# Moving three softmax normalisations on VectorE's list around the steps of a recurrence

## The chip, the cores and the metric

One core of one Trainium2 chip. The metric is the device time of one execution in microseconds (us); lower is better. The time before is the median of three runs, 133.39 us (132.92 to 133.72).

## The reference

Two branches run on separate inputs of 2048 tokens by 448 features, and their outputs are joined along the last axis. Branch A is dilated local attention with 16 heads of 28 features, a window of 8 keys at a step of 2. Branch B is a diagonal complex recurrence over the 2048 tokens, between two projections, with a skip product.

```python
def _A_ref(x, wqkv, wo):
    ...
    logits = jnp.where(mask[None, None, :, :], logits, -1e9)
    attn = _softmax(logits, axis=-1)
    o = jnp.einsum("bhsw,bhswd->bhsd", attn, vg)
    return (lambda x, *d: x.transpose(*d))(o, 0, 2, 1, 3).reshape(B, S, D) @ wo

def _B_ref(x, Lambda_re, Lambda_im, B_re, B_im, C_re, C_im, log_dt, Dskip):
    ...
    for t in range(L):
        h = Lam_bar[None, :] * h + Bu[:, t, :]
        hs.append(h)
    hseq = jnp.stack(hs, 1)
    y = 2.0 * jnp.einsum("blp,dp->bld", hseq, Cmat).real + x * Dskip[None, None, :]
    return y
```

## The kernel before

Tokens are handled in pairs (even, odd), so that 1024 pairs remain; they are cut into 8 blocks of 128 for the attention and into two halves of 512 for the recurrence. Every piece of work is a named step, and one hand-written string, `ORDER`, lists all steps in the order in which they are issued. A name ends in a letter for the engine (P TensorE, V VectorE, A ScalarE, G GpSimd, S SyncE's queue) and for many in the number of a PSUM unit, U0 to U3. Each engine works through its own steps strictly in the order of that string and waits, instruction by instruction, for what the data need. A step that stands later on an engine's list therefore cannot overtake one that waits. In the profile PE is TensorE, DVE VectorE, ACT ScalarE, POOL GpSimd and SP SyncE.

The steps that matter here:

- **Attention.** `s{b}{p}` are the logits of block b (lines 645 and 649; 655 and 661 for the block of borders, b = 8), `x{b}{p}` the exponential on ScalarE (671, 673), `a{b}{p}` the products with the values (680, 682), which end in a unit U0 or U1. `n{b}` on VectorE normalises: a reciprocal of the sums (691) and a product (692) that reads the PSUM unit and writes the tile O. Only then is the unit free for TensorE's next step in it. `ot{b}` is a DMA transposition of O on SyncE's queue (698, 701); `w{t}f` and `w{t}t` are the output projection (362, 360) from the transposed tile.
- **Recurrence.** `b{k}{h}` computes the input of component pair k in half h (727), `be` copies it to the tile u. `ri{k}{h}` rotates it on VectorE: two products with cosine and sine into ra and rb (742, 743), then a sum and a difference into rv (744, 745). `sc{k}{h}{i}` are two scans over rv into rs (755). `ro{k}{h}` rotates back into the tile h (764 to 767). ra, rb, rv and rs have one buffer each.
- **Output of B.** `g0`, `g1`, `g2` (782, 784) with `ge0`, `ge1`, `gp2` on ScalarE and `ge2` on VectorE (819) build the small matrix Gm. `xd{t}` on VectorE (841) writes the skip product, which reads the tile xo, into the PSUM unit to which `y{t}` on TensorE (851, 854) then adds. xo comes by two transfers that GpSimd issues in the step `xol` (908, 909), which stands in the string well ahead of its first reader, xd1.
- **GpSimd and ScalarE** scale rows of the second projection (`tc..`, line 534 on GpSimd), and `c..` on VectorE (540) adds the other half; GpSimd's next piece waits for a buffer that such a `c` step frees.

Between 47 us and the end of the attention VectorE's list runs, in the order of the string: n0, c24, ri00, n1, c23, c21, two scans, c22, n2, ro00, c25, ri20, and so on to n3, the c steps, ro20, ri11, n4, c26, sc110, n5, ge2, xd1, n8, sc111, xd0, ro11, ri21, sc210, n6. On TensorE the same stretch ends with y1, s61, y0, a60, a61, s70, w3t, w3f, w0f: w0f writes the unit that n6 reads.

The steps involved, in the code:

```python
rc = rcs[0:n, 2 * b:2 * b + 2, :]
av = U[u_][:, :, 0:29 * H].rearrange("p t (h c) -> p t h c", c=29)
V.reciprocal(rc, av[0:n, :, :, 28])
V.tensor_tensor(O[0:n, :].rearrange("p (t h d) -> p t h d", t=2, h=H), av[0:n, :, :, 0:DH],
                rc.unsqueeze(3).to_broadcast((n, 2, H, DH)), ALU.mult)
```

Of the kernel before, what the change touches and what calls it, by code (L numbers as in the profile page):

```python
# [10 lines left out]
ALU = mybir.AluOpType  # L11
# [6 lines left out]
HALF = 512  # L18
# [26 lines left out]
n8.V1 y1.P0 sc111.V ot8.S xd0.V1 ro11.V s61.P y0.P1 x61.A ri21.V ye1.A0 yo1.S oc0.A a60.P0 sc210.V ye0.A1 yo0.S a61.P0
s70.P n6.V0 w3t.P1 x70.A w3f.P1 sc211.V ot6.S w0f.P0 we3.A1 wo3.S ro21.V w0t.P0 oc1.A s71.P we0.A0 wo0.S w4f.P1 x71.A
ri31.V w5f.P0 w5t.P0 w4t.P1 sc310.V w1t.P2 we4.A1 wo4.S w2t.P3 w1f.P2 we5.A0 wo5.S xd3.V1 w2f.P3 ro31.V we1.A2 wo1.S
a70.P0 we2.A3 wo2.S a71.P0 xd2.V2 y3.P1 n7.V0 xd5.V3 ot7.S ri01.V y2.P2 ye3.A1 yo3.S sc010.V oc2.A sc011.V w6f.P0
# [105 lines left out]
def kernel(  # L154
# [17 lines left out]
    V, ACT, PE, G, SP = nc.vector, nc.scalar, nc.tensor, nc.gpsimd, nc.sync  # L172
# [6 lines left out]
    def t_(shape, dt, name, tag=None):  # L179
        return sb.tile(shape, dt, tag=tag or name, name=name)  # L180
# [5 lines left out]
    u = t_([128, 7, HALF], BF16, "u")  # L186
# [13 lines left out]
    tab = t_([128, 2, 4, HALF], BF16, "tab")  # L200
# [342 lines left out]
    for m in range(7):  # L543
        o = m % 4 if m != 3 else 3
# [165 lines left out]
    def hbuf():  # L710
        if "h" not in lazy:
            lazy["h"] = t_([128, 7, NP + 4], BF16, "h", "rB")
            V.memset(lazy["h"][:, :, 0:1], 0.0)
# [4 lines left out]
    rv = [t_([128, 2, HALF], BF16, f"rv{i}") for i in range(1)]
    rs = [t_([128, 2, HALF], BF16, f"rs{i}") for i in range(1)]
    for hf in range(2):  # L720
        for k in range(4):
            ms = (k, k + 4) if k < 3 else (3,)

            def f(e, u_, ms=ms, hf=hf):
                for j, m in enumerate(ms):
                    for i in range(7):
                        PE.matmul(U[u_][:, j, :], WT[:, i, 128 * m:128 * m + 128], xB[:, i, HALF * hf:HALF * hf + HALF], start=(i == 0), stop=(i == 6))  # L727
            step[f"b{k}{hf}"] = f

            def f(e, u_, k=k, ms=ms):  # L730
                if k < 3:
                    evac(e, u[:, k:k + 5:4, :], U[u_])
                else:
                    evac(e, u[:, 3, :], U[u_][:, 0, :])
            step[f"be{k}{hf}"] = f

            def f(e, u_, k=k, hf=hf):
                c, s = tab[:, 0, k, :], tab[:, 1, k, :]
                v = rv[0]
                if k < 3:  # L740
                    up = u[:, k:k + 5:4, :]
                    V.tensor_tensor(ra[:], up, c.unsqueeze(1).to_broadcast((128, 2, HALF)), ALU.mult)
                    V.tensor_tensor(rb[:], up, s.unsqueeze(1).to_broadcast((128, 2, HALF)), ALU.mult)
                    V.tensor_tensor(v[:, 0], ra[:, 0], rb[:, 1], ALU.add)
                    V.tensor_tensor(v[:, 1], ra[:, 1], rb[:, 0], ALU.subtract)
                else:
                    V.tensor_tensor(ra[:, 0], u[:, 3, :], c, ALU.mult)
                    V.tensor_tensor(ra[:, 1], u[:, 3, :], s, ALU.mult)
                    V.tensor_tensor(v[0:64, 0], ra[0:64, 0], ra[64:128, 1], ALU.add)
                    V.tensor_tensor(v[64:128, 0], ra[64:128, 0], ra[0:64, 1], ALU.subtract)  # L750
            step[f"ri{k}{hf}"] = f
            for i in range(len(ms)):
                def f(e, u_, k=k, hf=hf, i=i):
                    m = k + 4 * i
                    V.tensor_tensor_scan(rs[0][:, i], p["r2"][:, k:k + 1].to_broadcast((128, HALF)), rv[0][:, i],  # L755
                                         0.0 if hf == 0 else ini[:, m:m + 1], ALU.mult, ALU.add)
# [157 lines left out]
    flag = t_([1, 1], I32, "flag")  # L914
# [65 lines left out]
```

## Time and profile before

| | us |
|---|---|
| median of three runs | 133.39 |
| the profiled execution | 133.22 |
| its span, first to last instruction | 131.4 |
| TensorE busy | 124.2 |
| VectorE busy | 107.1 |
| ScalarE busy | 86.7 |
| GpSimd busy | 48.1 |

The profiled execution's time holds some 1.8 us outside the span. A row of the list in order of time reads: start, length, engine, line, operation, written tile and read tiles, shapes, number of instructions merged into the row; in brackets the idle time of the engine ahead of it and who ended that. A row of a window reads: its bounds and length, the busy time of each engine with its count of instructions, the granted clock of TensorE (1.00 in all windows shown), the share of the 16 DMA engines in use, and GB/s. A row on a transfer ends with its size and the time from issue to landing. Busy times of neighbouring rows overlap slightly, since instructions are pipelined.

### The profile page before, as it was taken

Reading aid. Unit: us, or ns where it says so; the run is one execution under the profiler, and the core shown is the slowest. Engines: PE = TensorE matmul, PEld = TensorE weight load, DVE = VectorE, ACT = ScalarE, POOL = GpSimd, SP = SyncE. Lnnn points to the kernel's source line nnn. Section 1 sums busy time; section 2 is a strip of 40 time slices with the busy share of each in tenths; the row PEclk is TensorE's granted clock in tenths of the full one; section 3 lists DMA queues with packets and bytes.
Section 4 is the critical chain, followed back from the end, with each engine's and each line's share of the span. In section 5 each row is a group of like instructions: output and inputs, shape, how many; then the busy total and the mean of one; then the engine's idle time right before and its main releaser. Section 6 shows DMA issues by size and latency. Waiting matters only on the chain.

```text
span 131.4 us, 3138 instructions
## 1 busy us (share of the span) xinstructions
PE 124.2 (94%) x1226; PEld 63.5 (48%) x1226; DVE 107.1 (81%) x225; ACT 86.7 (66%) x91; POOL 48.1 (37%) x75
## 2 busy tenths in 40 slices
PE   7999999999999999899999998799999999999970
PEld 2654443443444466454445556545644654445540
DVE  2467999999898999999998999999999999870000
ACT  3348878987999879968698967608697523222230
POOL 7998900799851906560077850000000000000000
PEclk9999999999999999999999999999999999999999
DMA  4999998899779995898879967990452652422222
GB/s 98 373 299 223 246 114 164 121 250 204 166 120 200 227 134 86 157 205 200 178 159 148 203 123 260 181 205 14 138 145 71 209 145 70 140 70 72 70 72 80
DMA packets 54594, 20.83 MB, mean 158 GB/s; under 512 B 46830, under 2 KB 54208, under 8 KB 54576
## 3 DMA queue, kind: packets, MB, share of 16 engines
q1 hardware_dynamic: 53424, 18.70, 68.1%
q0 software_dynamic: 656, 1.50, 4.1%
q10 hardware_dynamic: 496, 0.40, 0.9%
q8 instruction: 11, 0.18, 0.6%
q14 instruction: 7, 0.06, 0.2%
HBM read 5.30 MB, written 3.86 MB: 70 GB/s over the span
## 4 chain that ended last, share of the span: by engine, by line
PE 62%; DVE 23%; issue 5%; DMA 3%; POOL 2%; ACT 1%; SPq 0%; DVEq 0%
PE U L362 16%; PE U L851 11%; PE early L362 8%; PE U L727 6%; PE late L851 4%; PE U L854 3%; PE U L360 3%; DVE O L692 3%; DVE natW L540 3%; DMA Wt<-in_A_wqkv_dram 3%; DVE C L540 3%; DVE rs L755 2%; POOL wtmp L534 2%; PE late L362 2%; PE early L360 2%
## 5 line engine op out<-in xcount | busy, mean ns | idle before, releaser
L671 ACT ACTIVATE P<-s 128x1920 bf16<-128x1920 f32 (+1 forms) x16 | 28.6, 1785 | 5.7 <-PE s L649 5.6
L727 PE MATMUL U<-xB,WT 128*128 128x512 bf16 x98 | 22.3, 380 | 0.0
L362 PE MATMUL U<-Wt,xA 128*128 128x448 bf16 x90 | 19.9, 355 | 0.7 <-DVE O L692 0.4
L362 PEld LDWEIGHTS <-xA 128*128 128x128 bf16 x144 | 12.9, 98 | 14.9 <-issue 4.4
L335 ACT CAST ys<-U 128x896 bf16<-128x896 f32 (+1 forms) x11 | 9.5, 871 | 12.0 <-PE U L851 9.2
L534 POOL TENSOR_SCALAR wtmp<-CT,p_pah 128x448 f32<-128x448 bf16 x6 | 12.6, 2107 | 11.2 <-DVE natW L540 6.4
L851 PEld LDWEIGHTS <-h 128*128 128x128 bf16 x105 | 10.0, 98 | 9.2 <-DVE U L841 0.2
L727 PEld LDWEIGHTS <-WT 128*128 128x128 bf16 x98 | 9.2, 98 | 10.7 <-DMA xB<-in_B_x_dram 0.2
L362 PE MATMUL early<-Wt,xA 128*128 128x448 bf16 x54 | 11.8, 354 | 0.0
L335 ACT CAST u<-U 128x1024 bf16<-128x1024 f32 (+1 forms) x8 | 7.2, 905 | 4.6 <-PE U L727 4.5
L692 DVE TENSOR_TENSOR O<-U,rcs 128x896 bf16<-128x896 f32 (+1 forms) x9 | 9.8, 1091 | 0.3
L851 PE MATMUL U<-natW,h 128*128 128x448 bf16 x42 | 9.0, 353 | 0.1
L755 DVE TENSOR_TENSOR_SCAN rs<-p_r,rv 128x512 bf16<-128x512 f32 x7 | 9.0, 1304 | 0.0
L755 DVE TENSOR_TENSOR_SCAN rs<-p_r,ini,rv 128x512 bf16<-128x512 f32 x7 | 8.8, 1275 | 0.0
L680 PE MATMUL U<-Vt,P 128*128 128x29 bf16 x256 | 8.2, 176 | 0.6 <-DVE O L692 0.6
L680 PEld LDWEIGHTS <-P 128*128 128x128 bf16 x256 | 7.6, 96 | 2.0 <-issue 0.7
L335 ACT CAST ys<-late 128x896 bf16<-128x896 f32 (+2 forms) x6 | 4.3, 718 | 6.1 <-PE late L851 5.6
L362 PE MATMUL U<-wo,OT 128*128 128x448 bf16 x36 | 7.6, 353 | 0.0
L851 PE MATMUL U<-C,h 128*128 128x448 bf16 x35 | 7.4, 353 | 0.0
L534 POOL TENSOR_SCALAR wtmp<-CT,p_pag 128x448 f32<-128x448 bf16 x2 | 4.2, 2081 | 8.4 <-DVE C L540 8.4
L339 DVE COPY Wt<-Wt 64x1344 bf16<-64x1344 bf16 (+1 forms) x5 | 3.7, 736 | 4.1 <-DMA Wt<-in_A_wqkv_dram 4.1
L335 ACT CAST Nx<-U 128x896 bf16<-128x896 f32 x7 | 6.4, 908 | 1.0 <-PE U L360 1.0
(198 smaller groups left out, 233.9 us busy)
## 6 DMA issues: line engine op xcount, KB each, us to landing
out_dram<-ys SPq DMA_DIRECT2D x12, 224.0 KB, 2.5
tmpB<-in_A_x_dram SPq DMA_DIRECT2D x4, 224.0 KB, 3.6
xo<-in_B_x_dram POOLq DMA_DIRECT2D x1, 896.0 KB, 6.7
out_dram<-ys SPq DMA_DIRECT2D x7, 112.0 KB, 1.8
Wt<-in_A_wqkv_dram SPq DMA_DIRECT2D x1, 672.0 KB, 6.0
wo<-in_A_wo_dram SPq DMA_DIRECT2D x2, 336.0 KB, 4.4
natW<-in_B_B_re_dram SPq DMA_DIRECT2D x1, 336.0 KB, 6.0
natW<-in_B_B_im_dram SPq DMA_DIRECT2D x1, 336.0 KB, 7.3
```

Of the source, the lines that this page charges most:

```text
L335: ACT.copy(o, i)
L360: PE.matmul(ps(u_)[j], x()[r, 3, c], w()[r, 3], start=first, stop=not first, skip_group_check=True)
L362: PE.matmul(ps(u_)[j], x()[:, 4 * j + k, c], w()[:, 4 * j + k], start=(k == 0 and first), stop=(k == 2 and not first), skip_group_check=True)
L534: (G if e == "G" else V).tensor_scalar(view(held_t[name][:]), src(), scale(), None, ALU.mult)
L540: V.scalar_tensor_tensor(view(dst()), src(), scale(), view(t[:]), ALU.mult, ALU.add)
L671: ACT.activation(pv[:, :, :, c0:128], s4[:, :, 0:4 * n].rearrange("p g (s q) -> p g s q", s=4), ACTF.Exp, scale=SCALE)
L680: PE.matmul(U[u_][:, q, 29 * hd:29 * hd + 29], P[:, hd // 4, hd % 4, :], Vt[:, b, q, hd, :], start=(hd == 0), stop=(hd == H - 1), skip_gro ...
L692: V.tensor_tensor(O[0:n, :].rearrange("p (t h d) -> p t h d", t=2, h=H), av[0:n, :, :, 0:DH], rc.unsqueeze(3).to_broadcast((n, 2, H, DH)), ...
L727: PE.matmul(U[u_][:, j, :], WT[:, i, 128 * m:128 * m + 128], xB[:, i, HALF * hf:HALF * hf + HALF], start=(i == 0), stop=(i == 6))
L755: V.tensor_tensor_scan(rs[0][:, i], p["r2"][:, k:k + 1].to_broadcast((128, HALF)), rv[0][:, i], 0.0 if hf == 0 else ini[:, m:m + 1], ALU.m ...
L851: PE.matmul(ps[:, 0:D], hb[:, m, lo:lo + 128], C1()[:, m, :] if par else natW[:, m, 0:D], start=(m == 0 and par == 0), stop=(m == 6 and pa ...
L854: PE.matmul(ps[:, 0:D], xB[:, k, tk], Gm[:, k, :], start=False, stop=(k == 3), skip_group_check=True)
```

## The change

The string `ORDER` is changed at three places, and one step, ri00, is cut in two so that another can stand between its halves. On TensorE, ScalarE, GpSimd and SyncE the lists are the same as before, instruction for instruction; all that moves is on VectorE.

```diff
-s11.P tc23.G n0.V1 k5t.P0 x11.A k5f.P0 wtx2.S c24.V a10.P1 ri00.V tc21.G qt3.S ke5.A0 s20.P a11.P1 x20.A q7t.P0 xb1.S
-q7f.P0 n1.V1 s21.P qe7.A0 c23.V
+s11.P tc23.G n0.V1 k5t.P0 x11.A k5f.P0 wtx2.S c24.V a10.P1 rp00.V tc21.G qt3.S ke5.A0 s20.P a11.P1 x20.A q7t.P0 xb1.S
+q7f.P0 n1.V1 rq00.V s21.P qe7.A0 c23.V
...
-a41.P1 ge1.A0 s51.P ri11.V g0.P0 x51.A n4.V1
-s80.P ge0.A0 c26.V ot4.S a50.P1 sc110.V x80.A a51.P1 wol.S g2.P0 n5.V1 gp2.A0 s60.P ge2.V0 x60.A a80.P1 ot5.S xd1.V0
-n8.V1 y1.P0 sc111.V ot8.S xd0.V1 ro11.V
+a41.P1 ge1.A0 s51.P g0.P0 x51.A n4.V1 ri11.V
+s80.P ge0.A0 c26.V ot4.S a50.P1 x80.A a51.P1 wol.S g2.P0 n5.V1 gp2.A0 s60.P ge2.V0 x60.A a80.P1 ot5.S xd1.V0 n8.V1
+sc110.V xd0.V1 y1.P0 sc111.V ot8.S ro11.V
...
+            for nm, part in (("rp", 0), ("rq", 1)):
+                def f(e, u_, k=k, part=part):
+                    if part == 0:
+                        for o, s in ((ra, tab[:, 0, k, :]), (rb, tab[:, 1, k, :])):
+                            V.tensor_tensor(o[:], u[:, k:k + 5:4, :], s.unsqueeze(1).to_broadcast((128, 2, HALF)), ALU.mult)
+                    else:
+                        V.tensor_tensor(rv[0][:, 0], ra[:, 0], rb[:, 1], ALU.add)
+                        V.tensor_tensor(rv[0][:, 1], ra[:, 1], rb[:, 0], ALU.subtract)
+                step[f"{nm}{k}{hf}"] = f
```

The first place, on VectorE, is ri00 and n1 (O with number 862 is n1's output; after the change line numbers are higher by 1, and by 10 behind the new code). Before:

```order
L742 TENSOR_TENSOR ra<-u,tab 128x1024
L743 TENSOR_TENSOR rb<-u,tab 128x1024
L744 TENSOR_TENSOR rv_130<-ra,rb 128x512
L745 TENSOR_TENSOR rv_130<-ra,rb 128x512
L691 RECIPROCAL rcs<-U_94 128x32
L692 TENSOR_TENSOR O_862<-U_94,rcs 128x896
L540 SCALAR_TENSOR_TENSOR natW<-CT,p_sah,wtmp_124 128x448
```

And now, at the same place:

```order
L757 TENSOR_TENSOR ra<-u,tab 128x1024
L757 TENSOR_TENSOR rb<-u,tab 128x1024
L692 RECIPROCAL rcs<-U_94 128x32
L693 TENSOR_TENSOR O_860<-U_94,rcs 128x896
L759 TENSOR_TENSOR rv_130<-ra,rb 128x512
L760 TENSOR_TENSOR rv_130<-ra,rb 128x512
L541 SCALAR_TENSOR_TENSOR natW<-CT,p_sah,wtmp_124 128x448
```

The two instructions of n1 stand two places earlier, between the products and the sums of the rotation.

The second place, on VectorE, is ri11 and n4 (its output is O with number 1285, now 1281), followed by c26. Before:

```order
L742 TENSOR_TENSOR ra<-u,tab 128x1024
L743 TENSOR_TENSOR rb<-u,tab 128x1024
L744 TENSOR_TENSOR rv_130<-ra,rb 128x512
L745 TENSOR_TENSOR rv_130<-ra,rb 128x512
L691 RECIPROCAL rcs<-U_94 128x32
L692 TENSOR_TENSOR O_1285<-U_94,rcs 128x896
L540 SCALAR_TENSOR_TENSOR natW<-CT,p_sah,wtmp_125 128x448
```

And now:

```order
L692 RECIPROCAL rcs<-U_94 128x32
L693 TENSOR_TENSOR O_1281<-U_94,rcs 128x896
L743 TENSOR_TENSOR ra<-u,tab 128x1024
L744 TENSOR_TENSOR rb<-u,tab 128x1024
L745 TENSOR_TENSOR rv_130<-ra,rb 128x512
L746 TENSOR_TENSOR rv_130<-ra,rb 128x512
L541 SCALAR_TENSOR_TENSOR natW<-CT,p_sah,wtmp_125 128x448
```

n4 stands ahead of the whole rotation.

The third place, on VectorE, follows directly: the scan sc110 (first row before), n5 (O with number 1374, now 1373), ge2 (Gm), xd1 (U_93 from xo), n8 (the memset and O with number 1435, now 1434), sc111, xd0 (U_94 from xo), and the first product of ro11. Before:

```order
L755 SCALAR_TENSOR_TENSOR rs_131<-p_r_321,ini,rv_130 128x512
L691 RECIPROCAL rcs<-U_94 128x32
L692 TENSOR_TENSOR O_1374<-U_94,rcs 128x896
L819 TENSOR_TENSOR Gm<-U_93,part 64x448
L841 TENSOR_TENSOR U_93<-xo 128x448
L688 MEMSET O_1435 32x448
L691 RECIPROCAL rcs<-U_94 56x32
L692 TENSOR_TENSOR O_1435<-U_94,rcs 56x896
L755 SCALAR_TENSOR_TENSOR rs_131<-p_r_321,ini,rv_130 128x512
L841 TENSOR_TENSOR U_94<-xo 128x448
L764 TENSOR_TENSOR ra<-rs_131,tab 128x1024
```

And now:

```order
L692 RECIPROCAL rcs<-U_94 128x32
L693 TENSOR_TENSOR O_1373<-U_94,rcs 128x896
L829 TENSOR_TENSOR Gm<-U_93,part 64x448
L851 TENSOR_TENSOR U_93<-xo 128x448
L689 MEMSET O_1434 32x448
L692 RECIPROCAL rcs<-U_94 56x32
L693 TENSOR_TENSOR O_1434<-U_94,rcs 56x896
L765 SCALAR_TENSOR_TENSOR rs_131<-p_r_321,ini,rv_130 128x512
L851 TENSOR_TENSOR U_94<-xo 128x448
L765 SCALAR_TENSOR_TENSOR rs_131<-p_r_321,ini,rv_130 128x512
L774 TENSOR_TENSOR ra<-rs_131,tab 128x1024
```

The first scan has gone behind n8, and xd0 stands between the two scans, so that the second scan is now followed by the rotation that reads it.

More of the change, by code (lines that the diff above doesn't have):

```diff
@@ L37 @@
 k2f.P1 qe4.A0 sc100.V s10.P qt2.S ke2.A1 b00.P0 sc101.V x10.A kt2.S ro10.V tc24.G kt7.S a00.P1 be00.A0 a01.P1 wtx6.S
-s11.P tc23.G n0.V1 k5t.P0 x11.A k5f.P0 wtx2.S c24.V a10.P1 ri00.V tc21.G qt3.S ke5.A0 s20.P a11.P1 x20.A q7t.P0 xb1.S
-q7f.P0 n1.V1 s21.P qe7.A0 c23.V k6f.P1 x21.A c21.V tc22.G k6t.P1 sc000.V a20.P0 qt4.S ke6.A1 s30.P sc001.V a21.P0
-tc20.A kt6.S b20.P1 c22.V x30.A n2.V0 tc25.G kt4.S ro00.V kt5.S s31.P be20.A1 b11.P0 x31.A ot0.S c25.V ri20.V qt5.S
-b31.P1 be11.A0 qt6.S c20.V sc200.V s40.P be31.A1 vg1.S b01.P0 tc12.A tc16.V qt7.S x40.A c16.V c12.V tc15.G ot1.S
+s11.P tc23.G n0.V1 k5t.P0 x11.A k5f.P0 wtx2.S c24.V a10.P1 rp00.V tc21.G qt3.S ke5.A0 s20.P a11.P1 x20.A q7t.P0 xb1.S
@@ L42 @@
+q7f.P0 n1.V1 rq00.V s21.P qe7.A0 c23.V k6f.P1 x21.A c21.V tc22.G k6t.P1 sc000.V a20.P0 qt4.S ke6.A1 s30.P sc001.V
+a21.P0 tc20.A kt6.S b20.P1 c22.V x30.A n2.V0 tc25.G kt4.S ro00.V kt5.S s31.P be20.A1 b11.P0 x31.A ot0.S c25.V ri20.V
+qt5.S b31.P1 be11.A0 qt6.S c20.V sc200.V s40.P be31.A1 vg1.S b01.P0 tc12.A tc16.V qt7.S x40.A c16.V c12.V tc15.G ot1.S
 sc201.V tc10.A s41.P be01.A0 c10.V a30.P1 a31.P1 c15.V tc14.A b21.P0 vg2.S n3.V1 x41.A tc11.G c14.V ot3.S kb.G c11.V
-tc13.A s50.P ot2.S be21.A0 c13.V tc26.G a40.P1 ro20.V x50.A g1.P0 xol.G a41.P1 ge1.A0 s51.P ri11.V g0.P0 x51.A n4.V1
@@ L44 @@
-s80.P ge0.A0 c26.V ot4.S a50.P1 sc110.V x80.A a51.P1 wol.S g2.P0 n5.V1 gp2.A0 s60.P ge2.V0 x60.A a80.P1 ot5.S xd1.V0
[L45 to L48, printed above, removed]
@@ L49 @@
-ye2.A2 yo2.S ro01.V w6t.P0 w7t.P1 we6.A0 wo6.S w7f.P1 xda.V2 y5.P3 we7.V1 wo7.S gu1.V xd6.V0 gu2.P1 y6.P0 ye5.A3 yo5.S
-gu3.V1 xd4.V1 flag.V xdb.V3 y4.P1 ye6.A0 yo6.S ya7.P0 ye4.A1 yo4.S yb0.P2 ye7.A0 yb1.P3 yf0.A2 yf1.A3 yp7.A yq7.S
+tc13.A s50.P ot2.S be21.A0 c13.V tc26.G a40.P1 ro20.V x50.A g1.P0 xol.G a41.P1 ge1.A0 s51.P g0.P0 x51.A n4.V1 ri11.V
+s80.P ge0.A0 c26.V ot4.S a50.P1 x80.A a51.P1 wol.S g2.P0 n5.V1 gp2.A0 s60.P ge2.V0 x60.A a80.P1 ot5.S xd1.V0 n8.V1
+sc110.V xd0.V1 y1.P0 sc111.V ot8.S ro11.V s61.P y0.P1 x61.A ri21.V ye1.A0 yo1.S oc0.A a60.P0 sc210.V ye0.A1 yo0.S
@@ new lines @@
+a61.P0 s70.P n6.V0 w3t.P1 x70.A w3f.P1 sc211.V ot6.S w0f.P0 we3.A1 wo3.S ro21.V w0t.P0 oc1.A s71.P we0.A0 wo0.S w4f.P1
+x71.A ri31.V w5f.P0 w5t.P0 w4t.P1 sc310.V w1t.P2 we4.A1 wo4.S w2t.P3 w1f.P2 we5.A0 wo5.S xd3.V1 w2f.P3 ro31.V we1.A2
+wo1.S a70.P0 we2.A3 wo2.S a71.P0 xd2.V2 y3.P1 n7.V0 xd5.V3 ot7.S ri01.V y2.P2 ye3.A1 yo3.S sc010.V oc2.A sc011.V
+w6f.P0 ye2.A2 yo2.S ro01.V w6t.P0 w7t.P1 we6.A0 wo6.S w7f.P1 xda.V2 y5.P3 we7.V1 wo7.S gu1.V xd6.V0 gu2.P1 y6.P0
+ye5.A3 yo5.S gu3.V1 xd4.V1 flag.V xdb.V3 y4.P1 ye6.A0 yo6.S ya7.P0 ye4.A1 yo4.S yb0.P2 ye7.A0 yb1.P3 yf0.A2 yf1.A3
@@ L51 @@
+yp7.A yq7.S
 """
```

## The prediction

> **What bounds the kernel now.** I read the engine shares first, then VectorE's row of slices, then TensorE's list in order of time with its waits, and last VectorE's own list.
>
> ```profile
> span 131.4 us, 3138 instructions
> PE 124.2 (94%) x1226; PEld 63.5 (48%) x1226; DVE 107.1 (81%) x225; ACT 86.7 (66%) x91; POOL 48.1 (37%) x75
> DVE  2467999999898999999998999999999999870000
> ```
>
> TensorE (PE) is busy for 94% of the span, and VectorE (DVE) is full from about slice 4 to slice 34, that is up to some 112 us. Which of the two sets the end is read from TensorE's waits:
>
> ```profile
> 50.28 0.57 PE L680 MATMUL U<-Vt,P 128*128 128x29 bf16 x16
> 53.31 1.30 PE L362 MATMUL U<-Wt,xA 128*128 128x448 bf16 x6 [0.40 <-DVE O L692]
> 75.29 0.56 PE L680 MATMUL U<-Vt,P 128*128 128x29 bf16 x16
> 80.51 0.96 PE L680 MATMUL U<-Vt,P 128*128 128x29 bf16 x32 [0.56 <-DVE O L692]
> 83.67 1.06 PE L682 MATMUL U<-Vb,P 105*56 105x29 bf16 x32 [0.80 <-DVE O L692]
> 84.87 1.50 PE L851 MATMUL U<-natW,h 128*128 128x448 bf16 x7
> 94.04 2.60 PE L362 MATMUL U<-wo,OT 128*128 128x448 bf16 x12
> 97.39 2.44 PE L362 MATMUL U<-wo,OT 128*128 128x448 bf16 x12
> ```
>
> Three waits stand in brackets, 1.76 us in all, each for the product that ends a normalisation (line 692: n1, n4, n5). A fourth is hidden: the twelve products at 94.04 take 2.60 us, the twelve at 97.39 take 2.44. The group at 94.04 is w3f, six products, and then w0f, six products into bank U0, which n6 has to have read first. So w0f starts some 0.16 us late, and the cause is on VectorE:
>
> ```profile
> 93.83 0.33 DVE L691 RECIPROCAL rcs<-U 128x32 f32<-128x32 f32 x1
> 94.19 1.09 DVE L692 TENSOR_TENSOR O<-U,rcs 128x896 bf16<-128x896 f32 x1
> ...
> PEld L851 <- DVE U L841: 0.2, 1, 0.2
> ```
>
> n6 ends at 95.28. After that no wait of TensorE for VectorE shows up to the end (from 84 us on the view of waits has the 0.2 us at 84.87 alone), so the rest of the span, 131.4 - 95.3 = 36.1 us, is a fixed tail. Hence the time is set by when VectorE, working without a pause, gets through its list up to n6; the waits at 53, 80, 83 and 84 are slack that TensorE would meet again at w0f.
>
> **The change, part by part.** No instruction is added or removed; rows of VectorE's list change places, all of them before n6. The three parts are costed from these rows.
>
> ```profile
> 49.55 0.68 DVE L742 TENSOR_TENSOR ra<-u,tab 128x1024 bf16<-128x1024 bf16 x1
> 50.15 0.69 DVE L743 TENSOR_TENSOR rb<-u,tab 128x1024 bf16<-128x1024 bf16 x1
> 50.87 0.66 DVE L744 TENSOR_TENSOR rv<-ra,rb 128x512 bf16<-128x512 bf16 x1
> 51.79 0.34 DVE L691 RECIPROCAL rcs<-U 128x32 f32<-128x32 f32 x1
> ...
> 78.30 0.42 DVE L744 TENSOR_TENSOR rv<-ra,rb 128x512 bf16<-128x512 bf16 x1
> ...
> 49.73 2.30 POOL L534 TENSOR_SCALAR wtmp<-CT,p_pah 128x448 f32<-128x448 bf16 x1 [3.46 <-DVE natW L540]
> 57.68 1.40 POOL L534 TENSOR_SCALAR wtmp<-CT,p_pah 128x448 f32<-128x448 bf16 x1 [0.98 <-DVE natW L540]
> ```
>
> *n1 between the halves of ri00.* The sums that n1 reads end at 50.28 + 0.57 = 50.85, and rb ends at 50.84, so n1 can start at about 50.9 instead of 51.79. Its bank is free 0.9 us earlier, and the wait of 0.40 at 53.31 goes. For VectorE itself: the add that reads rb no longer follows it directly. From rb's start to the add's start there are 0.72 us; between ra and rb, where nothing depends, 0.60 (49.55 to 50.15), so a dependence costs 0.12 and one is saved. The add took 0.66 beside GpSimd's work of 49.73 to 52.03, where its like at 78.30 took 0.42; after the move it runs after 52.3, when that work is over, which is worth up to 0.24. The wait for the sums may give back 0.1. Bounds: -0.36 (all saved) to +0.3 (sums awaited, and both adds still stretched); I take -0.2, near the full sum less the wait.
>
> *n4 ahead of ri11.* n4's sums end at 75.29 + 0.56 = 75.85, well before VectorE comes there.
>
> ```profile
> 76.98 0.69 DVE L742 TENSOR_TENSOR ra<-u,tab 128x1024 bf16<-128x1024 bf16 x1
> 78.98 0.35 DVE L691 RECIPROCAL rcs<-U 128x32 f32<-128x32 f32 x1
> 79.37 1.09 DVE L692 TENSOR_TENSOR O<-U,rcs 128x896 bf16<-128x896 f32 x1
> 80.97 1.28 DVE L755 TENSOR_TENSOR_SCAN rs<-p_r,ini,rv 128x512 bf16<-128x512 f32 x1
> 82.16 0.33 DVE L691 RECIPROCAL rcs<-U 128x32 f32<-128x32 f32 x1
> 83.54 0.60 DVE L819 TENSOR_TENSOR Gm<-U,part 64x448 bf16<-64x448 f32 x1
> 84.17 0.63 DVE L841 TENSOR_TENSOR U<-xo 128x448 f32<-128x448 bf16 x1
> ```
>
> n4 starts at 76.98 instead of 78.98 and ends at 78.46 instead of 80.46. The sums at 80.51 no longer wait (0.56 gone), and they end at about 80.9, before VectorE's next normalisation at 80.97. The order of dependences is the same, so VectorE's own time is unchanged: nothing gained.
>
> *The scan sc110 behind n5, the sum for Gm, xd1 and n8.* The scan occupies 82.16 - 80.97 = 1.19 us of the list. n5, Gm's sum and the skip product xd1 all come 1.19 earlier: xd1 could start at 84.17 - 1.19 = 82.98, and y1, which waits for it at 84.87, at about 83.7. xd0 stays where it was, and now sc111 is followed directly by ro11, which reads it: one dependence more, +0.12, so it cancels the one saved at n1. Without anything else the sum is -0.2 - 0 + 0.12 = -0.1 us, and TensorE's gain of 1.2 us at y1 is lost at w0f, because n6 is not earlier.
>
> What is late next is the data of xd1. It reads xo, which GpSimd loads in two transfers (issue and landing):
>
> ```profile
> 75.69 0.97 POOL L908 DMA_DIRECT2D xo<-in_B_x_dram  x1
> 76.66 0.57 POOL L909 DMA_DIRECT2D xo<-in_B_Dskip_dram  x1
> ...
> xo<-in_B_x_dram POOLq DMA_DIRECT2D x1, 896.0 KB, 6.7
> xo<-in_B_Dskip_dram POOLq DMA_DIRECT2D x1, 112.0 KB, 6.1
> ...
> 80.48 1.23 SPq L698 DMA_TRANSPOSE OT<-O  x1
> ...
> 78.50:79.50 1.00, 1.00 (x21) 0.53 (x19) 0.96 (x4) 0.22 (x1) 0.00 (x0) 1.00 0.94 367
> 79.50:80.50 1.00, 0.45 (x36) 0.43 (x29) 1.00 (x2) 1.00 (x2) 0.00 (x0) 1.00 1.03 392
> 80.50:81.50 1.00, 0.99 (x34) 0.96 (x35) 1.00 (x2) 1.00 (x1) 0.00 (x0) 1.00 0.30 113
> 81.50:82.00 0.50, 0.50 (x8) 0.26 (x8) 0.50 (x1) 0.25 (x1) 0.00 (x0) 1.00 0.63 141
> 82.00:83.00 1.00, 0.87 (x24) 0.43 (x21) 0.96 (x3) 0.55 (x2) 0.00 (x0) 1.00 1.12 176
> ```
>
> They land at 75.69 + 6.7 = 82.39 and 76.66 + 6.1 = 82.76. Before, that left 1.4 us of slack ahead of xd1; now 82.98 - 82.76 = 0.2. And n4 triggers a transfer: the transposition ot4 on SyncE's queue, issued at 80.48, right behind n4. It is now issued at 78.5. In the windows (next to last number: the share of the 16 DMA engines) they are full with xo from 78.5 to 80.5, drop to 0.30, and fill again with ot4 about 1 us after its issue. Moved 2 us forward, ot4's packets come from 79.5 on, into xo. ot4 needs 0.5 x 0.63 + 1.12 = 1.4 us of all engines up to 83.0. By the mean share xo is almost through at 80.9, yet its second part lands at 82.76: the slowest engine ends well behind the mean, and ot4's share on that engine is interleaved too. Bounds for the delay of xo: 0 (it gives way to nothing) to 1.4 (all of ot4 goes ahead of its end). I take 1.1, nearer the upper end, since engines at 0.94 to 1.03 have no room. Then xo lands at 83.86, xd1 starts at about 83.9 instead of 82.98, and VectorE stands still for 0.9 us, with n8, the two scans, ro11, ri21 and n6 queued behind. n1's gain does not soften this: xo's issue follows GpSimd's work, which VectorE releases, and moves with it.
>
> The Trainium skill, page "DMA: Bandwidth & Descriptors", section "Queues, rings and completion order", says that each DMA engine takes turns between the queues that have work, a whole packet of several descriptors at a time. By it xo on GpSimd's queue and ot4 on SyncE's would share every engine and the delay would lie near the upper bound, 1.4 us; the windows above never have both in flight, so this trace cannot show it.
>
> **Sum.** -0.2 (n1) + 0.12 (dependence) + 0.9 (xd1 waits for xo) = +0.8 us on n6, and as much on w0f and the end. The profiled execution took 133.22 us (131.4 of span), 0.17 below the median 133.39. So I expect a span of 132.2, 134.0 for such an execution, and **134.2 us** as median. From the bounds: xo delayed by 0.5 gives +0.2, by 1.4 gives +1.1, with n1 at +0.3 instead of -0.2 it gives +1.6. The forecast's own range is 133.6 to 135.0.
>
> **Rivals.**
> *No change.* xo keeps its pace, lands by 82.8, and xd1 does not wait: -0.1 us, 133.3. For it: the share falls to 0.30 at 80.5, so there is room for half of ot4. Against it: 0.2 us of slack is little.
> *Faster: the stretched instructions go.* GpSimd's product took 2.30 at 49.73 and 1.40 at 57.68, so the two engines hinder each other. In the row
>
> ```profile
> 69.46 0.69 DVE L540 SCALAR_TENSOR_TENSOR C<-CT,p_sag,wtmp 128x448 bf16<-128x448 bf16 x1 [0.33 <-POOL wtmp L534]
> 55.50 1.51 DVE L755 TENSOR_TENSOR_SCAN rs<-p_r,rv 128x512 bf16<-128x512 f32 x1
> ```
>
> VectorE waits 0.33 for GpSimd, and a scan takes 1.51 where the one above takes 1.28. If n1's earlier place lets GpSimd finish sooner all along, 0.24 + 0.33 + 0.23 + 0.12 = 0.9 is gained, less 0.12: 132.6. It decides only if GpSimd's chain comes ahead of VectorE's; but VectorE releases each link of it (natW, L540), so both should move together. The Trainium skill, page "SBUF — State Buffer", on the shared port pair, says that a VectorE instruction with two SBUF inputs and a GpSimd one that reads SBUF exclude each other for a whole instruction; n1 reads PSUM, so by it GpSimd would get through beside n1, which speaks for the 0.24 and for no more.
> *Faster still: TensorE keeps its start at y1.* 1.2 us, 132.2. The late w0f speaks against it.
> *Slower in another way:* both adds of ri00 and c23 meet GpSimd's work and xo waits for all of ot4 and for the loads of wo, which SyncE issues right behind ot4 and so also earlier: some +1.6, 135.0.
> That the list does not change as it says is excluded by the order shown.
>
> **How the numbers follow.** Forecast (xo late) 0.55, no change 0.22, faster in the two ways 0.15, slower in another way 0.08. About 0.5%, 0.67 us, is what a measurement of this kernel can tell from no change. Of the forecast, 0.40 lies above +0.67 and 0.15 below; of no change 0.04 goes to faster, since the n1 term is open; of the faster cases 0.13 pass the bound. Slower 0.40 + 0.08 = 0.48; same 0.15 + 0.18 + 0.02 = 0.35; faster 0.04 + 0.13 = 0.17. The range is 132.5 to 135.0, which leaves out the last two rivals' far ends.
>
> **What would show it.** Right: w3f and w0f further apart than before (1 us or so instead of 0.16), no wait at 53 and 80, xd1 idle before its start with xo's transfer as releaser, xo's landing over 7 us from issue. Wrong: no idle time ahead of xd1, then no change; n6 earlier than 95.0, then the rows of GpSimd must tell why. A wait of TensorE for VectorE after w0f, or an n1 that waits past 51.0, would break the sum.

## The result and the profile after

| us | before | after |
|---|---|---|
| median, 21 executions each, in turn on one chip | 133.07 | 134.37 |
| lowest and highest | 132.91, 138.76 | 132.94, 139.84 |
| the profiled execution | 133.22 | 133.35 |
| its span | 131.4 | 131.6 |

The ratio of after to before is 1.0046, with a 95% interval of 1.0025 to 1.0066: +0.6 us. The interval lies clear of no change, but +0.6 is below the 0.67 us that the prediction named as the smallest step it could tell from none, so by that bound the time counts as the same. The ratio is smaller than the step between the medians because executions more than 1.5% above the fastest are left out of it, one of before and five of after, among them the three longest of the group of 11 described next.

The median hides how the times lie. The 21 executions of before stand between 132.9 and 133.8 but for one. Of those of after, 8 stand between 132.94 and 133.58, as before, and 11 between 134.1 and 135.2; the two last are further out. The profiled execution, 133.35, belongs to the lower group, so its profile shows the change *without* what makes the upper group. The share of executions between 134.0 and 135.5 is used below as a second measure.

First the engine shares of after:

```profile
span 131.6 us, 3138 instructions
PE 124.6 (95%) x1226; PEld 64.0 (49%) x1226; DVE 107.3 (82%) x225; ACT 86.7 (66%) x91; POOL 48.0 (37%) x75
```

Then TensorE's list in order of time and all its waits from 45 us on (engine and line that waited, whom for, total, times, longest):

```profile
52.84 1.31 PE L363 MATMUL U<-Wt,xA 128*128 128x448 bf16 x6
79.76 0.97 PE L681 MATMUL U<-Vt,P 128*128 128x29 bf16 x32
82.31 1.06 PE L683 MATMUL U<-Vb,P 105*56 105x29 bf16 x32
83.56 1.50 PE L861 MATMUL U<-natW,h 128*128 128x448 bf16 x7 [0.20 <-DVE U L851]
...
92.73 1.31 PE L363 MATMUL U<-wo,OT 128*128 128x448 bf16 x6
95.36 1.29 PE L363 MATMUL U<-wo,OT 128*128 128x448 bf16 x6 [1.32 <-DVE O L693]
97.41 2.44 PE L363 MATMUL U<-wo,OT 128*128 128x448 bf16 x12
```

```profile
PE U L363 <- DVE O L693: 1.3, 1, 1.3
PE U L861 <- DVE U L851: 0.2, 1, 0.2
PE U L728 <- DMA xB<-in_B_x_dram: 0.2, 1, 0.2
```

The three waits of before are gone, and y1 starts at 83.56 instead of 84.87. TensorE keeps these 1.31 us up to w3f (92.73 for 94.04). There they end: w0f, which the trace of before ran together with w3f as twelve products, is now a row of its own behind 1.32 us of idle time, released by n6 (line 693). The twelve products after that begin at 97.41; before it was 97.39. Four waits of 1.9 us in all became one of 1.32 and two of 0.2, and the start of the tail did not move (the whole span is 0.2 us longer). Busy time per engine alone would have hidden this: PE rose from 94 to 95%.

VectorE's list in the same execution:

```profile
50.89 0.36 DVE L692 RECIPROCAL rcs<-U 128x32 f32<-128x32 f32 x1
...
52.29 0.41 DVE L759 TENSOR_TENSOR rv<-ra,rb 128x512 bf16<-128x512 bf16 x1
...
80.77 0.36 DVE L692 RECIPROCAL rcs<-U 128x32 f32<-128x32 f32 x1
81.16 1.09 DVE L693 TENSOR_TENSOR O<-U,rcs 128x896 bf16<-128x896 f32 x1
...
82.87 0.63 DVE L851 TENSOR_TENSOR U<-xo 128x448 f32<-128x448 bf16 x1
...
87.21 1.27 DVE L765 TENSOR_TENSOR_SCAN rs<-p_r,ini,rv 128x512 bf16<-128x512 f32 x1
88.52 0.69 DVE L774 TENSOR_TENSOR ra<-rs,tab 128x1024 bf16<-128x1024 bf16 x1
...
94.22 1.09 DVE L693 TENSOR_TENSOR O<-U,rcs 128x896 bf16<-128x896 f32 x1
```

xd1 starts at 82.87, 1.30 earlier than before and with no idle time in brackets; n6's product starts at 94.22, before at 94.19. So here VectorE did the same work in the same time in another order. What xd1 reads had come in time. Its two loads and the transposition ot4 on the timelines of the two issuing queues:

```profile
75.46 0.97 POOL L918 DMA_DIRECT2D xo<-in_B_x_dram  x1
76.44 0.57 POOL L919 DMA_DIRECT2D xo<-in_B_Dskip_dram  x1
...
78.28 1.36 SPq L699 DMA_TRANSPOSE OT<-O  x1
```

And the same three in the view of transfers, each row ending with the time from issue to landing:

```profile
xo<-in_B_x_dram POOLq DMA_DIRECT2D x1, 896.0 KB, 6.1
xo<-in_B_Dskip_dram POOLq DMA_DIRECT2D x1, 112.0 KB, 5.4
OT<-O SPq DMA_TRANSPOSE x1, 4.4
```

xo landed at 76.44 + 5.4 = 81.8, although ot4 was issued beside it: sooner after its issue than before (6.1). By this execution the forecast delay does not exist: no idle time ahead of xd1 is the sign that the prediction gave for no change. The median of the 21 says otherwise, and the experiments ask which it is.

### The profile page after: what moved, and what is told of

Its sections match the earlier page's. It is cut to its first block, busy times and chain, and to the rows that moved or that the text cites. A ratio compares the mean times of both kernels' runs of the same rounds, so it can differ in the third digit from the quotient of the medians.

```text
span 131.6 us, 3138 instructions
## 1 busy us (share of the span) xinstructions
PE 124.6 (95%) x1226; PEld 64.0 (49%) x1226; DVE 107.3 (82%) x225; ACT 86.7 (66%) x91; POOL 48.0 (37%) x75
## 4 chain that ended last, share of the span: by engine, by line
PE 62%; DVE 28%; issue 3%; POOL 2%; ACT 0%; DVEq 0%
PE U L363 17%; PE early L363 8%; PE U L861 7%; PE U L728 6%; DVE O L693 5%; DVE rs L765 5%; PE late L861 4%; PE U L361 3%; DVE C L541 3%; PE U L864 2%; POOL wtmp L535 2%; PE x L509 2%; DVE natW L541 2%; PE U L681 2%; PE late L363 2%
## 5 line engine op out<-in xcount | busy, mean ns | idle before, releaser
L535 POOL TENSOR_SCALAR wtmp<-CT,p_pah 128x448 f32<-128x448 bf16 x6 | 13.6, 2275 | 12.3 <-DVE rv L746 6.8
L363 PEld LDWEIGHTS <-OT 128*128 128x128 bf16 x48 | 4.4, 98 | 6.2 <-issue 2.5
```

The costliest lines, as they stand in the source:

```text
L363: PE.matmul(ps(u_)[j], x()[:, 4 * j + k, c], w()[:, 4 * j + k], start=(k == 0 and first), stop=(k == 2 and not first), skip_group_check=True)
L535: (G if e == "G" else V).tensor_scalar(view(held_t[name][:]), src(), scale(), None, ALU.mult)
```

## The experiments

Theory X is the prediction's: VectorE's list sets the end, and the upper executions are those in which xd1 stands still for xo. Its rivals: ot4 is not what delays xo; TensorE's clock suffers from the new wait at w0f (T); or the moved steps cost VectorE something else. All executions, twelve of each kernel unless it says otherwise, beside executions of before on the same chip:

| kernel | median, us | before there, us | ratio and interval | 134.0 to 135.5 |
|---|---|---|---|---|
| after again, e1 | 133.58 | 133.49 | 1.0015 (0.9982 to 1.0049) | 2 |
| ot4 late, e2 | 133.66 | 133.49 | 1.0020 (0.9996 to 1.0044) | 4 |
| xo early, e3 (6) | 137.72 | 133.49 | 1.0113 (1.0070 to 1.0157) | 1 |
| products before w0f, e4 | 133.59 | 133.49 | 1.0012 (0.9991 to 1.0034) | 3 |
| n1 alone, e5 | 133.27 | 133.34 | 1.0001 (0.9979 to 1.0024) | 1 |
| all but n1, e6 | 133.80 | 133.34 | 1.0033 (1.0009 to 1.0056) | 3 |
| after again, e7 | 133.63 | 133.34 | 1.0008 (0.9987 to 1.0030) | 3 |
| after again, e8 | 133.50 | 133.34 | 1.0017 (0.9990 to 1.0043) | 3 |
| xo in three transfers, e9 | 133.11 | 133.04 | 1.0016 (0.9998 to 1.0035) | 1 |
| after, xo's issue late, e10 | 133.69 | 133.04 | 1.0027 (0.9999 to 1.0055) | 2 |
| before, xo's issue late, e11 | 133.08 | 133.04 | 1.0000 (0.9989 to 1.0011) | 0 |

Before itself had 2 of 114 executions between 134.0 and 135.5 (all four sets), after 11 + 2 + 3 + 3 = 19 of 57. So the upper group comes with the change and is not the spread of the chips alone (theory N in the expectations below).

**The changed kernel again (e1, e7, e8)**, without an edit, to get other executions into the profile.

> The changed kernel once more, for its single runs and for a second profile. In the profile at hand n6 ends at 95.31 us (95.29 before) and xo did not make xd1 wait, yet the median of 21 runs is 1.3 us higher, and single runs lie from 132.9 to about 135. Theory X (xo lands late in some of the executions, because ot4 shares the DMA engines with it): single runs again spread over 133.0 to 134.7, the median 0.3 to 1.3 above before; if the profile falls on a long execution, its xd1 starts 0.5 to 1.4 later than 82.87 with idle time ahead of it, and n6 ends as much later. Theory T (TensorE runs slower after the 1.3 us in which it now waits at w0f): the same spread, but n6 at 95.3 also in a long execution, and the products behind w0f take longer. Theory N (spread of the chip): before shows the same spread beside it.

> The changed kernel a third time, to catch a profile of an execution of the group above 134. If the transpositions held back by xo are the cause: ot4, ot5 or the one for OTb land several us after 82.7, 88.4 and 88.9, and a wait of ScalarE or TensorE for OT or OTb stands before w0f. If xB is the cause: the wait for xB at about 60 us is over 1 us. If TensorE's clock is: n6 at about 95.3 and slower products behind w0f.

> The changed kernel a fourth time, for the same reason and with the same expectations as the third.

The repeats came out nearer to before than the first measurement: each of their intervals takes in 1. The upper executions are there each time, but fewer (8 of 36 instead of 11 of 21). The profile of e7, an execution of 134.05, is one of them. Its transfers:

```profile
xo<-in_B_Dskip_dram POOLq DMA_DIRECT2D x1, 112.0 KB, 7.0
OT<-O SPq DMA_TRANSPOSE x1, 6.1
```

VectorE's list in e7:

```profile
82.25 0.60 DVE L829 TENSOR_TENSOR Gm<-U,part 64x448 bf16<-64x448 f32 x1
83.68 0.63 DVE L851 TENSOR_TENSOR U<-xo 128x448 f32<-128x448 bf16 x1 [0.83 <-DMA xo<-in_B_Dskip_dram]
...
95.02 1.09 DVE L693 TENSOR_TENSOR O<-U,rcs 128x896 bf16<-128x896 f32 x1
```

And w0f on TensorE in e7:

```profile
96.16 1.29 PE L363 MATMUL U<-wo,OT 128*128 128x448 bf16 x6 [1.32 <-DVE O L693]
```

This is the forecast in full: xo takes 7.0 us from issue, xd1 waits 0.83 for it, n6 is 95.02 - 94.22 = 0.80 later than in the profile of after, w0f 0.80, and the execution 134.05 - 133.35 = 0.70. That this execution differs from that one by xo is shown. How the transfer ended stands in the windows of e7 (busy time of each engine with its count, granted clock, share of the DMA engines, GB/s):

```profile
81.00:82.00 1.00, 0.93 (x26) 0.46 (x22) 0.97 (x2) 0.98 (x2) 0.00 (x0) 1.00 2.81 75
82.00:83.00 1.00, 0.75 (x34) 0.72 (x23) 0.85 (x2) 0.80 (x2) 0.00 (x0) 1.00 0.06 24
```

In the first the engines hold far more than they move: a share of 2.81, so several packets are open on one engine at once, and 75 GB/s. In the second the share is 0.06, about what one engine of 16 would give; the view does not say whether it is one, nor whose packets these are (the loads of wo were issued from 81.0 on). VectorE's pause from 82.85 to 83.68 begins in this stretch. In after's own profile the window from 81 to 82 reads 1.07 and 147 GB/s.

Ordered by xo, the three repeats and the first profile of the same kernel give 5.4, 5.6, 6.3 and 7.0 us for xo's second part, and 4.4, 4.5, 5.4 and 6.1 for ot4 (after, e1, e8, e7). They go up together. In before ot4, issued only when xo was within 2.3 us of landing, took 3.2. In the four executions xd1 waits for xo 0, 0, at most 0.15 (e8) and 0.83 us.

**ot4 out of xo's way (e2).**

```diff
-s80.P ge0.A0 c26.V ot4.S a50.P1 x80.A a51.P1 wol.S g2.P0
+s80.P ge0.A0 c26.V a50.P1 x80.A a51.P1 wol.S ot4.S g2.P0
```

> The changed kernel, with the transposition ot4 issued behind the four loads of wo instead of ahead of them, so that it cannot meet xo. Theory X: the spread upwards goes, median as before within 0.3 us (133.0 to 133.4), xo lands 5.5 us or less after its issue. Theory T and theory N: the same as the changed kernel beside it, 0.3 to 1.3 above before, since the wait at w0f stays 1.3 us.

The ratio is that of e1, and as many executions lie above 134.0 (four of twelve each). So taking ot4 away does not give back the time, and that part of theory X, that ot4 *is* the cause, is not borne out. The far end may differ: the highest of e2 is 134.43, while the four of e1 lie at 134.74 and above. But e4 below, which leaves ot4 in its new place, has only one of twelve above 134.5, so twelve executions do not settle it. The profile (134.10) shows a second way into the upper group. Two waits of TensorE in e2:

```profile
PE U L728 <- DMA xB<-in_B_x_dram: 0.4, 1, 0.4
PE U L792 <- ACT u L336: 0.3, 1, 0.3
```

The windows of e2 in which xo ends, and xo's landing:

```profile
80.00:81.00 1.00, 1.00 (x61) 0.96 (x54) 1.00 (x3) 1.00 (x2) 0.00 (x0) 1.00 0.20 78
81.00:82.00 1.00, 1.00 (x21) 0.59 (x17) 0.79 (x3) 1.00 (x1) 0.00 (x0) 1.00 0.04 15
```

```profile
xo<-in_B_Dskip_dram POOLq DMA_DIRECT2D x1, 112.0 KB, 6.4
```

VectorE in e2, at n5, xd1 and n6:

```profile
81.36 0.36 DVE L692 RECIPROCAL rcs<-U 128x32 f32<-128x32 f32 x1 [0.18 <-PE U L681]
...
83.47 0.63 DVE L851 TENSOR_TENSOR U<-xo 128x448 f32<-128x448 bf16 x1
...
94.81 1.09 DVE L693 TENSOR_TENSOR O<-U,rcs 128x896 bf16<-128x896 f32 x1
```

xd1 has no wait, yet n6 is 0.59 late. VectorE is late before xd1: TensorE stood 0.4 for the second half of xB at 60 us and 0.3 for ScalarE at 74 us, n4 starts at 77.11 instead of 76.77, and n5 now waits 0.18 for its sums, because n5 follows a51 directly. That the wait for xB alone makes n4 late is not shown: e1 has the same 0.4 and starts n4 at 76.85. And xo took 6.4 us from issue although the DMA engines were nearly empty for its last two microseconds (0.20 and 0.04): here no other transfer's packets held up its end.

**xo before GpSimd's product (e3).**

```diff
-tc13.A s50.P ot2.S be21.A0 c13.V tc26.G a40.P1 ro20.V x50.A g1.P0 xol.G a41.P1
+tc13.A s50.P ot2.S be21.A0 c13.V xol.G tc26.G a40.P1 ro20.V x50.A g1.P0 a41.P1
```

> The changed kernel, with the two transfers of xo issued ahead of GpSimd's last product instead of behind it, about 2.3 us earlier, so that they land at about 79.5 us, 3 us before xd1. Theory X: median as before within 0.3 us. Theory T and theory N: the same as the changed kernel, 0.3 to 1.3 above before.

Meant to give xo slack, it cost time: two of the six executions took 134.55 and 135.54 (the ratio of 1.0113, +1.5 us, goes by these), four took 137.5 to 138.2. The profile is of one of the four (137.46). VectorE and TensorE in it:

```profile
85.11 1.09 DVE L693 TENSOR_TENSOR O<-U,rcs 128x896 bf16<-128x896 f32 x1 [3.84 <-DMA OT<-O]
```

```profile
86.25 1.63 PE L683 MATMUL U<-Vb,P 105*56 105x29 bf16 x32 [3.97 <-DVE O L693]
87.82 2.79 PE L861 MATMUL U<-natW,h 128*128 128x448 bf16 x7
```

The shortest, median and longest time from issue to landing of the transpositions into OT between 70 and 90 us:

```profile
DMA to landing us min/median/max: 3.2/4.2/11.2
```

And the second part of xo:

```profile
xo<-in_B_Dskip_dram POOLq DMA_DIRECT2D x1, 112.0 KB, 9.5
```

And windows of e3; the granted clock is the third number from the end:

```profile
84.25:84.50 0.25, 0.00 (x0) 0.00 (x0) 0.00 (x0) 0.00 (x0) 0.00 (x0) 1.00 0.08 7
84.50:84.75 0.25, 0.00 (x0) 0.00 (x0) 0.00 (x0) 0.00 (x0) 0.00 (x0) 0.52 0.08 9
...
87.50:91.30 3.80, 3.80 (x19) 1.76 (x17) 3.70 (x6) 0.00 (x0) 0.00 (x0) 0.50 0.89 85
91.30:93.00 1.70, 1.70 (x10) 0.69 (x8) 1.67 (x2) 0.00 (x0) 0.00 (x0) 0.99 0.09 14
```

xo, issued at 73.0 and 74.0, now met the transposition ot2, issued at 73.8, and both lost: ot2 took 11.2 us to landing where 3.2 is the least, xo's second part 9.5. n5 writes the tile that this transposition reads, so VectorE stood 3.84 us, TensorE 3.97. From 84.5 to 91.3 us the granted clock was 0.50, and y1's seven products took 2.79 instead of 1.50. In this execution the overlap was expensive; it says nothing on xd1. How much of the four long executions is the edit's is open: before itself, on the same chip, had three of 29 at 136.9 to 138.1 with the same mean granted clocks of 0.975 and 0.987, and the two shorter executions of e3 have no profile.

**Products into w0f's gap (e4).** To test T, sixteen small products of ones go into columns 464 to 512 of unit U1, which nothing reads, ahead of w0f.

```diff
-w3f.P1 sc211.V ot6.S w0f.P0
+w3f.P1 sc211.V ot6.S fil.P1 w0f.P0
```

> The changed kernel, with 16 small products of constants on TensorE ahead of w0f, into columns of U1 that nothing reads, about 1 us of work in the 1.3 us in which TensorE waits there; they add nothing to the output. Theory T: the spread goes, median as before within 0.3 us. Theory X and theory N: the same as the changed kernel, 0.3 to 1.3 above before.

The sixteen products took only 0.56 us. The wait of w0f shrank to 0.92, so the gap became smaller but did not close, and the ratio stayed at that of e1. What decides is the clock. In after it is 1.00 right behind the wait:

```profile
95.00:97.00 2.00, 1.64 (x12) 0.70 (x15) 1.97 (x3) 0.37 (x3) 0.00 (x0) 1.00 0.22 45
```

T falls: 1.32 us without work did not touch the clock, and five of the 19 upper executions of the changed kernel, e7's among them, have a mean granted clock of 1.000 over their whole span.

**The parts apart (e5, e6).** e5 has the new order around n1 and the old one from n4 on; e6 the reverse.

```diff
-q7f.P0 n1.V1 s21.P qe7.A0 c23.V
+q7f.P0 n1.V1 rq00.V s21.P qe7.A0 c23.V
```

> The kernel before, with n1 between the halves of ri00 and nothing else moved. What is known: with the whole change VectorE comes to c23 0.22 us earlier, xo does not come late, and TensorE meets a second bound at 59.9 to 60.5 us, where it waits for the second half of xB; single runs of the whole change have a group at 134.1 to 135.2 that before has not. Theory B (the second half of xB paces TensorE and ScalarE, and through ScalarE's products VectorE, so that n1's 0.22 is given back by 69 us): median within 0.2 us of before; no group at 134.1 to 135.2, since no wait at w0f is made. Theory E (VectorE running 0.2 us earlier is what exposes it to ScalarE and GpSimd, and that makes the group): a group at 134.1 and above in a third of the runs.

> The kernel before, with n4, n5, ge2, xd1, n8 and xd0 moved as in the change, but n1 where it was. Theory B: n6 ends 0.1 us later than before (one dependence more), TensorE waits 1.2 to 1.4 us at w0f, median +0.1 (133.1 to 133.6), and, if the group above 134 comes from ot4 meeting xo or from the long wait at w0f, the group is here. Theory E: no group, median within 0.2 us of before.

In e5's profile (133.00) TensorE still waits for n4 at 80 us, and n6's product on VectorE is earlier:

```profile
80.28 0.96 PE L680 MATMUL U<-Vt,P 128*128 128x29 bf16 x32 [0.51 <-DVE O L692]
```

```profile
93.96 1.09 DVE L692 TENSOR_TENSOR O<-U,rcs 128x896 bf16<-128x896 f32 x1
```

93.96 for 94.19 is -0.23, and the execution is 133.22 - 133.00 = 0.22 shorter. That this comes so near the predicted n1 term is luck. VectorE starts ri00 in e5 at 49.46, in before at 49.55, so 0.09 is there before the moved step. From ri00's start to c23's start it is 52.95 - 49.46 = 3.49 instead of 53.18 - 49.55 = 3.63, so n1's move itself gains 0.14. And e11 below, with n1 in its old place, has n6's product at 93.97 as well. Over twelve executions the gain is lost in the spread (1.0001); one of them lies in the upper group, not the third that theory E expects. The interval of e6 lies above 1, which points to the second and third part as the place of the loss; but the intervals of e5 and e6 overlap, and e7 and e8, the whole change on the same chip, have 1.0008 and 1.0017. The profile of e6 (133.95), though, caught lateness from upstream and not from xo: xd1 had no wait, and n5 waited for late sums (VectorE's waits):

```profile
DVE rcs L692 <- PE U L681: 0.2, 1, 0.2
```

**xo in three transfers (e9).** The skip weights come first, then blocks 0 and 1, which xd1 and xd0 read, then the rest.

```diff
-Q[e].dma_start(xo[:, 0:8, :], B_x[0].rearrange(...)[:, :, D:2 * D])
+xs = B_x[0].rearrange(...)[:, :, D:2 * D]
...
+Q[e].dma_start(xo[:, 0:2, :], xs[:, 0:2])
+Q[e].dma_start(xo[:, 2:8, :], xs[:, 2:8])
```

> The changed kernel, with xo loaded in three transfers instead of two: the skip weights first, then the two blocks that xd1 and xd0 read, then the other six; the same bytes. Theory X (in part of the executions xd1 waits for xo, up to 0.8 us seen, and n6 and the end come as much later): the two transfers that xd1 needs land before 81 us in every execution, xd1 never waits, the runs above 134.5 go (3 to 4 of 12 before), and the median is within 0.2 us of before. Theory C (the upper runs come from the wait at w0f or from xB): the runs above 134.5 stay.

The profile (132.79) shows the wanted slack, in GpSimd's timeline (issue of the blocks 0 and 1), the transfers, and xd1 on VectorE:

```profile
76.12 0.73 POOL L920 DMA_DIRECT2D xo<-in_B_x_dram  x1
```

```profile
xo<-in_B_x_dram POOLq DMA_DIRECT2D x1, 224.0 KB, 4.8
xo<-in_B_Dskip_dram POOLq DMA_DIRECT2D x1, 112.0 KB, 3.7
```

```profile
82.73 0.63 DVE L851 TENSOR_TENSOR U<-xo 128x448 f32<-128x448 bf16 x1
```

What xd1 needs landed at 76.12 + 4.8 = 80.9, 1.8 us ahead of it. One of twelve executions lies in the upper group, for 19 of 57 without the split, and none above 134.5: as theory X expects. But the changed kernel without the split was not run on this chip, and the ratio of 1.0016 is no lower than that of the repeats, so it is not proof that the waits for xo made the upper group.

**xo issued later, in after and in before (e10, e11).** Two clearings of a spare tile on GpSimd ahead of the issue.

```diff
+for _i in range(2):
+    G.memset(wait_t[:], 0.0)
```

> The changed kernel, with two fills of an unused tile on GpSimd ahead of the two transfers of xo, which delay their issue by about 1.25 us. Theory X: xd1 has 0.2 us of slack at best, so it waits 0.3 to 1.9 us in nearly every execution, n6 ends at 95.6 to 97.2, median 0.8 to 1.5 above before. Theory C: the same as the changed kernel, 0.1 to 0.6 above before.

> The kernel before, with the same two fills ahead of the transfers of xo. Theory X: there xd1 stands 1.2 us later and has 1.4 us of slack, so it waits at most 0.3 us and the median is within 0.3 us of before. If the fills cost something by themselves (GpSimd and VectorE share ports), it shows here.

The delay came out at 0.9 to 1.0 us, less than meant. Before took it without harm: 133.08, and none of twelve over 133.36. After, with as much, has 133.69, and 8 of twelve over 133.36. In the profile that was taken of after even so, xd1 did not wait: xo needed only 5.3 us from an issue at 77.46 and landed at 82.8, and xd1 began at 83.06. Before agrees with theory X: it has slack ahead of xd1. After does not: X expected a wait in nearly every execution and 0.8 to 1.5 us, and the ratio is +0.4 us, with an interval that takes in no change, beside +0.1 to +0.2 for the repeats; theory C expected 0.1 to 0.6. As the changed kernel without the delay was not run on this chip, 8 of twelve over 133.36 cannot be put down to the delay either: e7 and e8 have 8 of twelve each without it.

**n6 ahead of sc210 (e12)**, with the split of e9, to take away w0f's wait as well.

```diff
-a60.P0 sc210.V ye0.A1 yo0.S a61.P0 s70.P n6.V0 w3t.P1
+a60.P0 n6.V0 sc210.V ye0.A1 yo0.S a61.P0 s70.P w3t.P1
```

> The changed kernel with xo split as above, and with n6 also moved ahead of the scan sc210, where its sums are ready (they end at about 92 us). n6 then ends 1.28 us earlier, at about 94.0, and w0f follows. If the time is set by VectorE's list up to n6, as the prediction has it: w0f starts at about 94.1 instead of 95.34, TensorE meets ro01 next (its end at 112.8 stays, and y5, which reads it, started at 113.38 before), so 0.5 us is gained and about 0.7 of the 1.2 is waited away at y5: span 130.8 to 131.1, median 132.4 to 132.9, 0.4 to 0.8 below before. If the front of TensorE were fixed in another way: no gain.

404.5 us: a slip in the edit. In that place n6 also comes ahead of a61 and reads the unit without the second half of its sums; the kernel's own guard on the sums then computes the attention a second time on an exact path, whose tiles are named e_. One of its rows in the list of the costliest groups (count, busy us and mean ns, then idle us):

```profile
L103 DVE TENSOR_TENSOR e_pr<-e_q,e_k 128x7168 bf16<-128x7168 bf16 x8 | 31.1, 3885 | 77.1 <-DMA e_k<-e_k 52.3
```

The other executions do not have these steps, and the span is 403 us with them. It says nothing of the question. The edit meant, sc210 moved behind n6 with n6 left where it is, was not tried, so whether a version beats both kernels stays open.

## Why the prediction was right, and where a size was off

**The bound** held. VectorE's list up to n6 sets the end: TensorE's 1.31 us at y1 were lost at w0f to the last 0.02 (95.36, against 94.04 + 1.30 = 95.34). The rival that TensorE keeps its start at y1 falls with it. Waits of TensorE for VectorE after w0f, which would have broken the sum, do not occur. Other executions follow n6 too: beside the profile of after, n6 is 0.02, 0.18, 0.19, 0.58, 0.59, 0.71 and 0.80 later in e8, e10, e1, e4, e2, e6 and e7, and the time is 0.02, 0.28, 0.29, 0.46, 0.75, 0.60 and 0.70 longer. It is not all: in e9 n6 is 0.15 earlier and the time 0.56 shorter.

**The number** came out right in part by luck. The prediction gave one time for a kernel that has two groups of executions. In the first measurement 13 of 21 lay above 134.0, so the median of 134.37 fell near 134.2. In the three repeats (e1, e7, e8) it was 133.50 to 133.63, which is nearer to the rival of no change (133.3).

**n1, -0.2:** measured -0.14 between ri00 and c23, in after (52.95 - 49.46) as in e5. The add that stood beside GpSimd's work took 0.41 instead of 0.66, as argued: it starts at 52.29, after that work (49.63 + 2.30 = 51.93). The other rival, that GpSimd's whole chain gains 0.9, does not show.

**n4, 0:** its wait at 80 us went, and n4's move by itself changed nothing on VectorE. But the third part brought n5 directly behind a51: in e2, e4, e6 and e10 n5 waits 0.2 for sums that are late. The prediction saw that VectorE's next normalisation comes about as the sums end (80.9 and 80.97) and gave it no price.

**The dependence, +0.12:** measured within after: from sc111's start to that of ro11 it is 88.52 - 87.21 = 1.31, where before xd0 followed the scan after 88.00 - 86.81 = 1.19. Another 0.1, which the prediction does not have, lies between n5 and xd1: from n5's reciprocal to xd1 it is 82.87 - 80.77 = 2.10 now and was 84.17 - 82.16 = 2.01. So from ri00's start to n6's product VectorE takes 94.22 - 49.46 = 44.76 us after and took 94.19 - 49.55 = 44.64 before, one execution each, +0.1 where the sum of the terms without xo was -0.1.

**xd1 waits for xo, +0.9:** the mechanism is right, the term was sized as a constant and is not one. The step that failed is "xo is delayed by 1.1": xo's second part takes between 5.4 and 7.0 us from issue in four executions of one kernel, 0 to 0.83 us of wait for xd1. Against the 6.1 of before that is a delay of -0.7, -0.5, +0.2 and +0.9. The slack was judged from one landing (82.76) as if it were the landing. In e7 the term is the predicted 0.8 to 0.9, in the three other profiles of this kernel it is 0 or nearly so. In the first measurement the ratio gives +0.6, in the repeats +0.1 to +0.2, within "no change". The predicted time of 134.2 is about that of an execution with the wait (e7, 134.05), 133.3 that of one without, and both occur.

**That ot4 delays xo** was the reason given for the delay, and it is half right. ot4 beside xo takes 4.4 to 6.1 us instead of 3.2, and grows as xo does, which fits that the two get in each other's way. The Trainium skill, page "DMA: Bandwidth & Descriptors", section "Queues, rings and completion order", has each DMA engine take turns between queues with work; by that both should lose, and e7's two landings (7.0 and 6.1) agree. But xo also took 5.1, 5.7 and 6.1 with ot4 in its old place (e5, e11, before), and 6.4 in e2, where ot4 comes only after xo has landed; in the seven profiles with ot4 in the new place and xo in two parts (e3 apart) it took 5.3 to 7.0. The prediction says that the windows of before never have both in flight. They do: ot4 is issued at 80.48, by the prediction's own reading it fills the engines from about 81.5, and xo lands at 82.76. What decides between 5.4 and 7.0 in a given execution is open, as is what share of the upper group of the first measurement is xo's and what share is lateness from upstream, since both were seen (e7; e2 and e6) and none of those executions has a profile.

## What to carry to other kernels

Here, work moved about within a full in-order list did not bring the list's end forward: the waits that vanished from the other engine came back, added up, at the place where that engine next needed the list's last item. What such a move changes is slack, so look at everything that was ready "in time" for the steps that come earlier, transfers first, and compare the slack with the spread of a landing over several executions, not with one landing. If it is too little, the transfer can be cut so that its first reader waits only for its own part: in e9 that part landed 1.8 us ahead of its reader. That this makes the kernel faster is not shown.

## What was not expected of the hardware

A transposition and a GpSimd-issued load that meet can both wait, and long: 11.2 and 9.5 us to landing in one execution of e3, where 3.2 us is the least for such a transposition and 5.4 to 7.0 is what the load took in the four of the changed kernel. A transfer can land a microsecond after the engines have gone nearly idle: in e2 xo landed at 82.16 after a microsecond with a share of 0.04, in e7 at 83.53, with 0.06 from 82 to 83. And idle time did not always cost the clock: 1.32 us left it at 1.00. In e3 TensorE stopped at 86.25 - 3.97 = 82.28, the clock fell to about half at 84.5, 2.2 us later, and it was back at 91.3, 5.0 us after the work began again. The Trainium skill, page "TensorE: Matmul & The Clock Gate", section "What's actually happening", gives at least one window of about 3.4 us for each of the two, and has the windows run on their own, not from the start of the work. The return after 5.0 us agrees with that. The fall after 2.2 us came sooner, in one execution, and there the measurement decides.
